# A fused attention and FFT-gate kernel: 128-row position tiles, a forward DFT in four column groups, and six fixed load buffers

## The chip, the cores and the metric

One core of one Trainium2 chip. The metric is the device time of one execution in microseconds (us), lower is better. The kernel before took 247.44 us (median of 3 runs, 246.96 to 247.74). Runs labelled slow (1.5% or more above the fastest of the same kernel) are left out of every ratio.

Engines: PE is TensorE, DVE is VectorE, ACT is ScalarE, POOL is GpSimd, SP is SyncE. PE, DVE and ACT compute, POOL issues the loads from HBM, and SP issues stores and DMA transposes. PSUM is the memory that PE writes its results to, and copying a result out of it is called an eviction. The granted clock is the share of PE's full clock that the profile shows it was given.

## The reference, cut to what matters

```python
# 8 batches, 8 heads, 576 positions, 64 features a head, model width 512
q_p, k_p = phi(q), phi(k)              # relu(x) * (cos, sin) of the position
kv  = k_p^T v ; z = sum(k_p)           # per batch and head, 128 x 64
att = (q_p kv) / (q_p z + 1e-6)        # [576, 512] a batch
x1, x2, x3 = att @ w_proj, split       # 512 -> 3 x 512
y   = x1 * irfft(rfft(x2) * rfft(filter)) * x3     # along the 576 positions
out = y @ w_out
```

The kernel works through the batches with two or three of them in flight. One batch in the words of the traces: load q, k, v; `kp`, `qp` (phi, on DVE) and `va` (a copy of v, on ACT); `kv`; `qpt` (q_p transposed, so that PE can use it as weights); `num` and `att`; `fx` (the first stage of the DFT); `xt` (att transposed); `x2`; `dft`; `x0`/`x2` of the gate, from `xt`; `inv`, `y`, `out`. The moment at which the `kv` of a batch starts is the milestone that I use throughout. Batches are counted from 0.

## The kernel before: the parts that matter

Two tensors have to be transposed in every batch. Batches 0 and 1 do it on PE, with evictions by ACT and DVE. Later batches use DMA transposes, issued by SP:

```python
XT_DMA = (2, 3, 4, 5, 6, 7)     # batches whose xt is a DMA transpose
DMA_QT = 2                      # first batch whose qpt is one
# ... in emit_qt(b, hp), four calls a batch
if b >= DMA_QT:
    nc.sync.dma_start_transpose(out=..., in_=qp[...])       # 2 heads
    return
# ... otherwise PE transposes into PSUM, then an ACT and a DVE copy
# ... in emit_fx: the batch that is not in XT_DMA gets xt from extra matmuls
for dst, gs in ((fx, slice(0, 12)), (xt_t.get(b), slice(12, 24))):
    if gs.start and b in XT_DMA:
        continue
```

Loads go to a rotating pool of four buffers of 96 rows with 6 slots of 64. A load waits for the reader of the tile four loads back:

```python
rw = work.tile([NP, NH, NJ * D], FP16, tag="raw", bufs=4, name=f"{nm}raw{b}")
# ... k and v: one DMA each; q of batch 2 and later: three DMAs
```

The DFT of a batch is nine matmuls of 96 output rows. The last batch evicts its five output tiles in pieces to ACT and DVE, and both SP and ACT issue the stores.

Of the kernel before, what the change touches and what calls it, by code (L numbers as in the profile page):

```python
# [17 lines left out]
def kernel(  # L18
# [25 lines left out]
    NJ, NP = 6, 96  # L44
    NT = 6
# [11 lines left out]
    R3 = math.sqrt(3.0) / 2.0  # L57
# [11 lines left out]
    ccol = consts.tile([128, NJ], FP32, tag="ccol", name="ccol")  # L69
    scol = consts.tile([128, NJ], FP32, tag="scol", name="scol")  # L70
    tcol = consts.tile([128, NJ], FP32, tag="tcol", name="tcol")
    tcol_m = consts.tile([128, NJ], FP32, tag="tcol_m", name="tcol_m")
    epsc = consts.tile([128, NT], FP32, tag="epsc", name="epsc")
    ident = consts.tile([NP, NP], FP16, tag="ident", name="ident")
    swap = consts.tile([NP, NP], FP16, tag="swap", name="swap")
    half_pi = consts.tile([128, 1], FP32, tag="half_pi", name="half_pi")
    m_half_pi = consts.tile([128, 1], FP32, tag="m_half_pi", name="m_half_pi")
    m_pi = consts.tile([128, 1], FP32, tag="m_pi", name="m_pi")
    m_half = consts.tile([128, 1], FP32, tag="m_half", name="m_half")
    wr_col = consts.tile([128, 1], FP32, tag="wr_col", name="wr_col")  # L80
    fm = consts.tile([128, 24, 8], FP16, tag="fm", name="fm")
    tre = consts.tile([NP, 3, NP], FP16, tag="tre", name="tre")
    tim = consts.tile([NP, 3, NP], FP16, tag="tim", name="tim")


    tpad = [consts.tile([128, NP], FP16, tag=f"tpad{i}", name=f"tpad{i}") for i in range(7)]


    ire = consts.tile([NP, 4, QS], FP16, tag="ire", name="ire")
    iim = consts.tile([NP, 4, QS], FP16, tag="iim", name="iim")  # L90
    h3 = consts.tile([NP, 3, 3, DM], FP16, tag="h3", name="h3")
    wp16 = consts.tile([128, NC, 3 * DM], FP16, tag="wp16", name="wp16")
    wo16 = consts.tile([128, NC, DM], FP16, tag="wo16", name="wo16")
# [3 lines left out]
    qpt_buf = [consts.tile([128, NH * S], FP16, tag=f"qpt{i}", name=f"qpt{i}") for i in range(1)]  # L97
    va_buf = [consts.tile([NP, NH, NJ, 66], FP16, tag=f"va{i}", name=f"va{i}") for i in range(2)]
# [4 lines left out]
    def tsc(out, in0, s1, op0, s2=None, op1=None):  # L103
        if op1 is None:
            return nc.vector.tensor_scalar(out=out, in0=in0, scalar1=s1, scalar2=None, op0=op0)
        else:
            return nc.vector.tensor_scalar(out=out, in0=in0, scalar1=s1, scalar2=s2, op0=op0, op1=op1)  # L107

# [14 lines left out]
    XT_DMA = (2, 3, 4, 5, 6, 7)  # L123
    DMA_QT = 2

    def load_qk(b, nm, hs=slice(0, NH)):
        src = {"q": q, "k": k, "v": v}[nm]
        if hs.start == 0:
            rw = work.tile([NP, NH, NJ * D], FP16, tag="raw", bufs=4, name=f"{nm}raw{b}")
            raw_t[(b, nm)] = rw  # L130
        rw = raw_t[(b, nm)]
        view = src[b, hs].rearrange("h (p j) d -> p h (j d)", j=NJ)
        if nm == "q" and b >= DMA_QT:
            nc.gpsimd.dma_start(out=rw[:, hs, 0 : 3 * D], in_=view[:, :, 0 : 3 * D])
            for x in range(2):
                nc.gpsimd.dma_start(
                    out=rw[x::2, hs, 3 * D : 6 * D], in_=view[1 - x :: 2, :, 3 * D : 6 * D]
                )
        else:
            nc.gpsimd.dma_start(out=rw[:, hs], in_=view)  # L140
# [36 lines left out]
    def emit_iotas(part):  # L177
        if part == 0:
            iota("p_i", [128, 1], lambda t: [(t, [[1, 1]], 0, 1)])
            iota("s6_i", [128, NJ], lambda t: [(t, [[1, NJ]], 0, 6)])  # L180
            iota("orow_i", [128, 16], lambda t: [(t, [[1, 16]], 0, 0)])
            iota("nrow_i", [NP, NP], lambda t: [(t, [[1, NP]], 0, 0)])
            return
        iota("fr_i", [NP, 3, NP], lambda t: [
            (t[:, 0], [[3, NP]], 0, 0),
            (t[:, 1], [[6, 48], [4, 2]], 1, 0),
            (t[:, 2], [[6, 48], [2, 2]], 2, 0),
        ])
        iota("sg_i", [NP, NP], lambda t: [(t, [[0, 48], [-2, 2]], 1, 0)])
        iota("s3_i", [128, 3], lambda t: [(t, [[1, 3]], 0, 3)])  # L190
        iota("sr_i", [NP, QS], lambda t: [
            (t[:, ds(j * 48, 48)], [[12, 2], [192, 3], [24, 8]], 2 * j + 1, 0) for j in range(3)
        ])

    def emit_cols():
        p = cc["p"] = small("p")
        nc.vector.tensor_copy(out=p, in_=cc["p_i"])
        nc.vector.memset(half_pi, PI / 2.0)
        nc.vector.memset(m_half_pi, -PI / 2.0)
        nc.vector.memset(m_pi, -PI)  # L200
        nc.vector.memset(m_half, -FX / 2.0)
        nc.vector.memset(warm, 0.0)
        for t in tpad:
            nc.vector.memset(t, 0.0)
        sj = cc["s6_i"]
        nc.scalar.activation(out=ccol, in_=sj, func=AF.Sin, scale=-(PI / 2.0) / S, bias=half_pi)
        nc.scalar.activation(out=scol, in_=sj, func=AF.Sin, scale=(PI / 2.0) / S)
        nc.vector.reciprocal(out=tcol, in_=ccol)
        nc.vector.tensor_tensor(out=tcol, in0=tcol, in1=scol, op=AL.mult)
        tsc(ident, cc["nrow_i"], p[0:NP], AL.is_equal)  # L210
        par = cc["par"] = small("par")
        rnd(par, p, 0.5, -0.25)
        nc.vector.scalar_tensor_tensor(
            out=par, in0=par, scalar=-2.0, in1=p, op0=AL.mult, op1=AL.add
        )
        dest = small("dest")
        nc.vector.scalar_tensor_tensor(
            out=dest, in0=par, scalar=-2.0, in1=p, op0=AL.mult, op1=AL.add
        )
        tsc(dest, dest, 1.0, AL.add)  # L220
        tsc(swap, cc["nrow_i"], dest[0:NP], AL.is_equal)

    def emit_cols_m():
        cm = small("cm", NJ)
        sm = small("sm", NJ)
        nc.vector.tensor_copy(out=sm, in_=cc["s6_i"])
        off = small("off")
        tsc(off, cc["par"], -12.0, AL.mult, 6.0, AL.add)
        tsc(sm[:, 3:6], sm[:, 3:6], off, AL.add)
        nc.scalar.activation(  # L230
            out=cm, in_=sm, func=AF.Sin, scale=-(PI / 2.0) / S, bias=half_pi
        )
        nc.scalar.activation(out=tcol_m, in_=sm, func=AF.Sin, scale=(PI / 2.0) / S)
        nc.vector.reciprocal(out=cm, in_=cm)
        nc.vector.tensor_tensor(out=tcol_m, in0=tcol_m, in1=cm, op=AL.mult)

    def emit_pads():
        for va in va_buf:
            nc.vector.memset(va[:, :, :, D : D + 2], 1.0 / A1)

    def emit_fm():

        p = cc["p"]
        side = small("side")
        tsc(side, p, NP / 2 - 0.5, AL.is_gt)
        loc = small("loc")
        tsc(side, side, -2.0, AL.mult, 1.0, AL.add)
        tsc(loc, p, -(NP - 1) / 2.0, AL.add)
        nc.vector.tensor_tensor(out=loc, in0=loc, in1=side, op=AL.mult)
        tsc(loc, loc, (NP - 1) / 2.0, AL.add)  # L250
        li = small("li")
        rnd(li, loc, 1.0 / 8.0, -7.0 / 16.0)
        lo = small("lo")
        nc.vector.scalar_tensor_tensor(
            out=lo, in0=li, scalar=-8.0, in1=loc, op0=AL.mult, op1=AL.add
        )


        row = small("row")
        tsc(row, lo, 12.0, AL.mult)  # L260
        nc.vector.scalar_tensor_tensor(
            out=row, in0=li, scalar=96.0, in1=row, op0=AL.mult, op1=AL.add
        )
        pos = small("pos", NT)
        for t in range(NT):
            tsc(pos[:, t : t + 1], row, float(6 * (t % 2) + t // 2), AL.add)
        tsc(pos, pos, -(S - 1) / 2.0, AL.add)
        tsc(pos, pos, side, AL.mult, (S - 1) / 2.0, AL.add)
        tsc(pos, pos, float(S - 1), AL.min, 0.0, AL.max)
        nc.scalar.activation(out=epsc, in_=pos, func=AF.Sin, scale=-(PI / 2.0) / S, bias=half_pi)  # L270
        nc.vector.reciprocal(out=epsc, in_=epsc)
        tsc(epsc, epsc, EPS, AL.mult)
        orow_i = cc["orow_i"][:, 0:8]
        match = small("match", 8)
        nc.vector.tensor_copy(out=match, in_=orow_i)
        tsc(match, match, lo, AL.is_equal)

        coef = small("coef", 24)
        ph = small("ph", 6)
        for sl, (kk, c0) in enumerate([(0, 0.25), (3, 0.25), (1, 0.25), (1, 0.0), (2, 0.25), (2, 0.0)]):  # L280
# [30 lines left out]
            op=AL.mult,  # L311
        )

    NCOL = 3 * HS

    FX = 65536.0

# [720 lines left out]
```

## Time and profile before

| | before |
|---|---|
| time, median of the first three runs | 247.44 us |
| span of the profiled run | 242.4 us |
| granted PE clock, mean | 0.991 |
| kv of batch 2 / 3 / 7 starts | 67.8 / 91.3 / 188.2 us |
| steady batch, kv to kv | 24.21 us |
| last gate ends / last eviction ends | 231.93 / 238.42 us |

The prediction below shows the busy lines, the stages and the chain of a steady batch. In the timeline of a DMA queue the columns are start, time until the last of the group was issued, queue, line, operation, tiles and how many. Time in which the queue waits between two transposes of a group is counted in.

```profile
47.89 34.62 SPq L555 DMA_TRANSPOSE qpt<-qp  x8
82.56 3.57 SPq L633 DMA_TRANSPOSE xt<-att  x1
```

The first line covers eight q transposes, four of batch 2 and four of batch 3, with a break of 7.3 us between the fours. The same view, asked for each four alone (from 47.5 to 64 and from 70 to 82.54 us):

```profile
47.89 15.55 SPq L555 DMA_TRANSPOSE qpt<-qp  x4
70.78 11.73 SPq L555 DMA_TRANSPOSE qpt<-qp  x4
```

One of the eight takes 1.3 to 6.2 us in the queue, 3.3 on average. The median of all 24 in that run is 1.585 us. Nobody waited for those eight: PE's table of waits has no line with a DMA in it. The windows of the kernel show columns: width, busy us of PE, PEld, DVE, ACT and POOL with instruction counts, granted clock, mean share of the 16 DMA engines, GB/s; a share over 1 means that packets of several queues overlap.

### The profile page before, as it was taken

To read this page: it belongs to the slowest core of one execution; us is meant where nothing else is said; L and a number is where in the kernel's file an instruction comes from. 1 tells how busy PE (TensorE), PEld (TensorE's weight loads), DVE (VectorE), ACT (ScalarE), POOL (GpSimd) and SP (SyncE) were. 2 spreads that over 40 slices of the span, in tenths; PEclk is the share of its full clock that TensorE was granted. 3 is DMA by queue.
4 is the path that set the end of the run, shared out by engine and by line. 5 is a ranking of instruction groups with operands and counts; after the bars stand their busy time and mean duration, and the time that the engine had idled before them with its cause. 6 is when DMAs were issued, how large, how long until landed. Compare 5 with 4: busy or idle time off the path is not lost.

```text
span 242.4 us, 6225 instructions
## 1 busy us (share of the span) xinstructions
PE 218.4 (90%) x2333; PEld 151.2 (62%) x2333; DVE 212.3 (88%) x747; ACT 178.8 (74%) x275; POOL 35.3 (15%) x61
## 2 busy tenths in 40 slices
PE   1197897998988999999999999999999999999991
PEld 0066576655565866686668666866686668645840
DVE  7588999899889999999999999999999597729781
ACT  2354689999897974899488948894889488778731
POOL 8713411330401031002300230010000000000000
PEclk9998899999999999999999999999999999999999
DMA  5999999799999959999999999999495524063315
GB/s 69 158 205 205 205 208 188 110 162 171 146 202 156 167 92 223 158 153 159 208 249 173 144 194 254 192 142 194 107 187 101 153 54 91 5 171 94 106 42 174
DMA packets 76238, 37.39 MB, mean 154 GB/s; under 512 B 55088, under 2 KB 71856, under 8 KB 76208
## 3 DMA queue, kind: packets, MB, share of 16 engines
q0 software_dynamic: 26000, 16.85, 51.2%
q1 hardware_dynamic: 49792, 19.56, 43.0%
q10 hardware_dynamic: 416, 0.59, 0.8%
q8 instruction: 18, 0.29, 0.5%
q14 instruction: 12, 0.10, 0.1%
HBM read 33.69 MB, written 9.44 MB: 178 GB/s over the span
## 4 chain that ended last, share of the span: by engine, by line
PE 76%; ACT 11%; DVE 6%; DMA 4%; issue 1%; POOL 1%; ACTq 0%; POOLq 0%
PE x L713 26%; PE x L648 12%; PE out L785 11%; PE dft L680 6%; PE kv L543 4%; PE num L584 4%; PE fx L611 3%; PE inv L750 3%; PE inv L749 3%; ACT va L145 3%; DMA vraw<-in_v_dram 3%; DVE att L594 2%; PE out L803 2%; PE qt L563 2%; PE num L535 1%
## 5 line engine op out<-in xcount | busy, mean ns | idle before, releaser
L713 PE MATMUL x<-xt,wp 128*128 128x288 f16 x512 | 67.3, 286 | 0.0
L713 PEld LDWEIGHTS <-wp 128*128 128x128 f16 x512 | 48.9, 98 | 13.2 <-issue 0.4
L648 PE MATMUL x<-wp,fx 128*128 128x512 f16 (+1 forms) x160 | 35.4, 381 | 2.2 <-DVE qpt L569 1.6
L666 ACT ACTIVATE x2f<-x 128x1024 f16<-128x1024 f32 (+1 forms) x24 | 21.2, 885 | 17.1 <-PE x L648 17.1
L594 DVE TENSOR_TENSOR att<-num,rcp 96x768 f16<-96x768 f32 x32 | 30.4, 948 | 0.4
L785 PE MATMUL out<-wo,y 128*128 128x512 f16 (+1 forms) x132 | 30.3, 379 | 0.0
L723 ACT CAST x3s<-x 128x576 f16<-128x576 f32 x32 | 20.4, 638 | 8.5 <-PE x L713 8.0
L145 ACT COPY va<-vraw 96x768 f16<-96x768 f16 x24 | 18.7, 844 | 8.8 <-DMA vraw<-in_v_dram 8.8
L685 ACT CAST xf<-dft 96x1024 f16<-96x1024 f32 x24 | 24.1, 1005 | 1.3 <-PE dft L680 1.1
L543 PE MATMUL kv<-va,kp 96*128 96x65 f16 x384 | 16.1, 196 | 9.8 <-ACT va L145 7.9
L626 ACT CAST fx<-fx 128x576 f16<-128x576 f32 x32 | 20.5, 640 | 5.5 <-PE fx L611 5.5
L720 ACT CAST x1s<-x 128x576 f16<-128x576 f32 x32 | 20.5, 639 | 2.3 <-PE x L713 1.1
L543 PEld LDWEIGHTS <-kp 96*128 96x128 f16 x384 | 14.1, 99 | 12.6 <-DVE kp L107 10.9
L648 PEld LDWEIGHTS <-fx 128*128 128x128 f16 (+1 forms) x160 | 12.7, 100 | 14.8 <-issue 2.5
L584 PEld LDWEIGHTS <-qpt 128*128 128x128 f16 (+1 forms) x384 | 16.8, 106 | 8.2 <-issue 3.8
L785 PEld LDWEIGHTS <-y 128*128 128x128 f16 (+1 forms) x132 | 12.4, 98 | 14.6 <-issue 0.8
L738 DVE TENSOR_TENSOR g<-x3s,x1s 128x288 f16<-128x288 f16 x64 | 17.5, 298 | 4.3 <-ACT x3s L723 4.2
L688 DVE TENSOR_TENSOR m<-xf,h 96x1024 f16<-96x1024 f16 x24 | 16.4, 683 | 4.8 <-ACT xf L685 4.5
L764 DVE TENSOR_TENSOR eo<-eq 128x288 f16<-128x288 f16 x64 | 17.5, 299 | 2.5 <-ACT eq L753 2.5
L611 PE MATMUL fx<-fm,att 96*128 96x96 f16 x240 | 16.3, 207 | 3.6 <-DVE att L594 1.8
L584 PE MATMUL num<-kvs,qpt 128*128 128x65 f16 (+1 forms) x384 | 17.5, 200 | 1.9 <-DVE rcp L593 1.1
L611 PEld LDWEIGHTS <-att 96*128 96x128 f16 x240 | 13.6, 98 | 7.8 <-DVE att L594 3.5
(197 smaller groups left out, 422.1 us busy)
## 6 DMA issues: line engine op xcount, KB each, us to landing
out_dram<-os SPq DMA_DIRECT2D x61, 96.0 KB, 2.4
kraw<-in_k_dram POOLq DMA_DIRECT2D x7, 576.0 KB, 10.3
vraw<-in_v_dram POOLq DMA_DIRECT2D x7, 576.0 KB, 8.8
qraw<-in_q_dram POOLq DMA_DIRECT2D x8, 288.0 KB, 7.5
qraw<-in_q_dram POOLq DMA_DIRECT2D x12, 144.0 KB, 7.9
wp<-in_moe_w_proj_dram POOLq DMA_DIRECT2D x3, 512.0 KB, 11.6
out_dram<-os SPq DMA_DIRECT2D x22, 64.0 KB, 2.6
out_dram<-os SPq DMA_DIRECT2D x14, 48.0 KB, 3.1
```

Source lines behind the costliest of these rows:

```text
L145: copy(out=va_buf[b % 2][:, hs, :, 0:D], in_=raw_t[(b, "v")][:, hs].rearrange("p h (j d) -> p h j d", j=NJ),)
L543: nc.tensor.matmul(u[:, h // 4, ds((h % 4) * 65, 65)], kp[:, j, h].rearrange("p a b -> p (a b)"), va[:, h, j, 0:65], start=(j == 0), stop= ...
L584: nc.tensor.matmul(u[0:m, hh, ds(t * 65, 65)], qpt[:, c0 : c0 + 2 * m - 1 : 2], kvs[:, h // 4, ds((h % 4) * 65, 65)], start=True, stop=True,)
L594: mark["att", b, hp] = nc.vector.tensor_tensor(out=att[:, :, ds(hp * 128, 128)].rearrange("p t (h d) -> p h t d", h=2), in0=nv[:, :, :, 0: ...
L611: nc.tensor.matmul(dst.rearrange("p (g e o) -> p g e o", e=2, o=8)[:, :, e], att[:, 2 * j + e, ds(c * 128, 128)], fm[0:NP, gs], start=True ...
L626: mark["fx", b] = nc.scalar.copy(out=dst[:, c].rearrange("p g (j o) -> p j g o", j=3), in_=uf[:, 0:768].rearrange("p (j g o) -> p j g o", ...
L648: nc.tensor.matmul(dst, fx[:, c].rearrange("p g o -> p (g o)")[:, ds(128 * ch, n)], wp16[:, c, ds(DM, DM)], start=(c == cs[0]), stop=(c == ...
L666: mark["x2f", b, bl] = nc.scalar.mul(out=x2f[:, 2 * bl : 2 * bl + n], in_=u[:, 0:n], mul=X2SC)
L685: mark["xf", b, bl] = nc.scalar.copy(out=xf, in_=u[0:NP])
L713: nc.tensor.matmul(u[:, hf, 0:HS], wp16[:, i, ds(w * DM + c * 128, 128)], xt[:, i, ds(6 * hf, 6)].rearrange("p a b -> p (a b)") if b not i ...
L720: mark["x1s", b, c] = nc.scalar.copy(out=x1s, in_=us[0][:, :, 0:HS])
L785: nc.tensor.matmul(us[t], y[:, c, ds(OT[t], nr)], wo16[:, c], start=(c == 0), stop=(c == NC - 1),)
```

## The change

All position tiles become 128 rows: four slots of 128 and a fifth of 64. Tiles of 96 rows leave a quarter of PE's and DVE's rows unused. So `kv` and `num` need 40 matmuls for 48, and DVE needs ten `kp` steps for twelve. The forward DFT becomes matmuls of 32 output rows, four of which run side by side in PE's column groups. Six fixed buffers replace the pool of four, so loads can run further ahead. And `xt` of batch 1 becomes a DMA transpose, which takes work from ACT in the stage where ACT was full. The core of the diff:

```diff
-    XT_DMA = (2, 3, 4, 5, 6, 7)
+    raw_n = [0]
+    XT_DMA = (1, 2, 3, 4, 5, 6, 7)
+    raw_buf = [const(f"raw{i}", [128, NH, NJ * D], FP16) for i in range(6)]
 ...
-            rw = work.tile([NP, NH, NJ * D], FP16, tag="raw", bufs=4, name=f"{nm}raw{b}")
+            raw_t[(b, nm)] = raw_buf[raw_n[0] % len(raw_buf)]
+        nc.gpsimd.dma_start(              # four slots, runs of 1024 bytes
+            out=rw[:, hs, 0 : 4 * D],
+            in_=src[b, hs, 0:NM].rearrange("h (p j) d -> p h (j d)", j=4),
+        )
+        nc.gpsimd.dma_start(              # fifth slot, runs of 256 bytes
+            out=rw[0:64, hs, 4 * D : 5 * D], in_=src[b, hs, NM:S].rearrange("h p d -> p h d")
+        )
 ...
+            for comp, tab, c0 in ((0, fcos, 0), (1, fsin, 32)):
+                for x in range(4):
+                    nc.tensor.matmul(u[ds(32 * x, 32), comp, 0:n], st, mv, start=True, stop=True)
 ...   # last batch: all tiles up to the last column group, then the last one
+            emit_out(b - 1, OG, range(3))
+            emit_out(b - 1, OG, range(3, 4))
```

## The prediction

> **What bounds the kernel now.** I read the page's busy lines first, then the table of windows cut by stage, then the chain of waits inside one batch, then the start and the end in the timeline. The stretches are mine: the first gate starts at 30 us, ACT is saturated to 62, a steady batch runs from kv to kv (24.2 us).
>
> ```profile
> PE 218.4 (90%) x2333; PEld 151.2 (62%) x2333; DVE 212.3 (88%) x747; ACT 178.8 (74%) x275; POOL 35.3 (15%) x61
> ...
> 37.50:45.00 7.50, 5.91 (x89) 4.45 (x87) 7.50 (x23) 7.50 (x13) 0.77 (x1) 1.00 1.33 180
> 52.00:62.00 10.00, 8.68 (x73) 5.07 (x72) 10.00 (x29) 10.00 (x17) 0.88 (x1) 1.00 1.38 180
> 67.00:74.00 7.00, 5.09 (x115) 4.34 (x112) 6.35 (x24) 6.63 (x11) 0.02 (x1) 1.00 1.46 185
> 115.60:139.80 24.20, 24.20 (x271) 17.08 (x272) 23.55 (x75) 19.15 (x29) 3.54 (x6) 1.00 1.22 193
> 232.00:242.40 10.40, 5.19 (x28) 1.90 (x25) 4.30 (x10) 1.69 (x4) 0.00 (x0) 0.94 0.44 126
> ```
>
> The columns after the width are the busy us of PE, PEld, DVE, ACT, POOL. Three regimes. In a steady batch PE is busy 24.20 of 24.20 with DVE only 0.65 behind. From 37 to 62 us ACT and DVE are full and PE waits. In the last 10 us nobody is busy: that is latency. So 88% busy DVE is worth nothing in the middle and something at the start. The chain inside a steady batch prices PE's work:
>
> ```profile
> 115.60 1.63 PE kv L543 x48
> 117.23 1.73 PE x L648 x8
> 118.96 0.80 PE num L584 x24
> ...
> 121.88 0.66 PE dft L680 x3
> 122.54 0.40 PE num L584 x12
> 122.94 0.55 PE x L648 x4
> 123.50 0.78 PE dft L680 x3
> 124.27 1.96 PE x L713 x16
> 126.23 0.65 PE dft L680 x3
> 126.89 0.26 PE fx L611 x6
> ...
> 135.80 3.46 PE out L785 x16
> 139.25 0.56 PE out L803 x8
> ```
>
> No wait lies between these pieces; they add to 24.2. A 512-column matmul costs 0.216, one of 288 0.122, one of 65 about 0.033.
>
> **What the Trainium skill says, and the trace.**
> (1) "TensorE: Matmul & The Clock Gate", section Back-to-back issue gap: a warm stream costs columns over 2.4 GHz plus 2.5 ns. 512 gives 215.8 ns; the trace has 3.46/16 = 216. Agrees, so I use it for the new widths, 144 (62.5 ns), 160 (69) and 128 (56).
> (2) "TensorEngine Tiling (Array Packing)", Key Properties: tiles run independently, and changing the tiling mode drains TensorE. The last x2 block shows both: four 512-column matmuls in two column groups took 0.55, not 0.86, but above the 0.43 of two; and the next DFT block took 0.78 where its sisters take 0.66. So each change of mode costs about 0.12 us in this trace. No part of this kernel yet runs four groups.
> (3) "DMA: Bandwidth & Descriptors", Specifications: at least 512 B for line rate. The change cuts a k or v row run from 1536 B to 1024 B plus runs of 256 B. What that costs no run here shows.
>
> **The change part by part.**
>
> *PE, per steady batch.* kv and num go from 48 to 40 matmuls each: 8 x 0.032 and 8 x 0.033, -0.26 and -0.26. fx keeps 24 matmuls but they widen from 96 columns to 144 (16 of them) and 160 (8): 4 x (4 x 0.0625 + 2 x 0.069) = 1.55 against 4 x 0.26 = 1.04, +0.51. inv: 16 of 144 and 8 of 288 for 32 of 144, 1.98 for 2.00. Gate, x2 and out keep their columns. DFT: 9 matmuls of 512 (1.95 without the drain) become 16 of 512 and 8 of 128 with 32 columns of weights each. If four groups do run together the array time is 0.43 + 0.43 for the two large blocks, plus the second half of a block that the scheduler splits (below) 0.22, plus about 0.2 for the small one, some 1.25. But the instruction order built for the changed kernel puts two cosine matmuls, then the last ten num matmuls, then the other six: it splits the first block. Mode changes per batch rise from 4 to 10, 6 x 0.12 = +0.72. So -0.70 + 0.72: nothing. The split has a reason: the first block now reads four x2f chunks, so both evictions; before it read two chunks. The second eviction (1.03 us) begins when the last x2 matmul ends; num (0.33), two DFT (0.45) and num (0.33) cover 1.1 us of about 1.35. I charge +0.2. Sum: -0.26 - 0.26 + 0.51 - 0.02 + 0.02 + 0.2 = +0.2 per batch, over five steady batches and the last +1.0 us. The steady stage does not gain.
>
> *DVE, per batch.* kp 12 to 10 operations (2 x 0.26 at issue rate): -0.5; qp: relu 2 x 0.47 to 1 x 0.75 and 6 to 5 scales, -0.45; att 768 to 640 elements at 948 ns: 4 x -0.13 = -0.5; DFT products on three blocks of 1024 to two and one of 256, about -1.2; g one operation for two, 4 x -0.14; the y product split in two, 4 x +0.18. About -2.6 of 23.5. Hidden behind PE there, not at the start.
>
> *ACT, 31 to 62 us.* This is a queue without a gap (DVE too). In issue-rate cost, what disappears: the four xt copies of batch 1, now a DMA transpose, 4 x 0.53 = 2.1; filter-table evictions 6 x 0.5 + 0.5 to 2 x 0.92 + 0.4, -1.2; the third xf, -0.6; va of batches 1 and 2, 8 x -0.13 = -1.0; the extra inverse row, -0.3; and sines now placed ahead of the gate, -2.0. ACT falls from 31 to about 24. PE in the same stretch: h from 27 to 12 large matmuls plus 72 small ones of about 0.03, -1; fx of batch 1 8 x 0.26 to 4 x 0.39, -0.5; kv and num -0.5; 27 becomes 25. DVE 31 becomes 25 to 26 (the itl table adds 8 x 0.2). So the three limits lie at 24 to 26 and the stretch should end near 57 to 58 rather than 62.4. I take -5. From 67 to 74 the y chain and the att operations on DVE bind: +0.7 and -0.5; the batch after has 17.0 PE in 17.4. I add -0.8 for smaller DVE backlog.
>
> *0 to 30 us.* Each load is two DMAs, POOL issues one in 0.67, and there are more iotas ahead of v: v is issued about 1 us later, and v releases the first va at 8.9. Against it, DVE no longer stands behind an ACT sine that itself stood behind that va (2.47 idle), and the kp loop has ten steps for twelve. But scheduled order now has the second half's q scaling before the first att, and five sines before the last xt copy. I take 0, with 1.3 either way.
>
> *The end.* Before, the groups run one after another after the last y, 15 stores in 48-row pieces alternate on two queues, and ACT, which also issues stores, idles 3.85 before one half and 0.87 before the next. After, only the last c is left when y is done at about 233.7: four matmuls and one packed pair, 1.2 us; five 0.4 DVE evictions with ACT beside; five or six stores whose last is issued near 237, plus 2.3 to land. -2.3 us.
>
> Sum: +1.0 - 5.0 - 0.8 + 0 - 2.3 = -7.1, against the measured 247.4: 240.3.
>
> **The rivals.**
> *Four groups do not overlap.* Then the DFT is 16 x 0.216 + 8 x 0.056 = 3.9 instead of 1.95 and each batch gains 2 to 2.7: the kernel goes to about 255. For it: no four-group run in this trace. Against it: the two-group evidence, and out's packed 256-column matmuls, 0.56 for eight where serial would be 0.87.
> *DMA becomes the bound.* Loads rise from 3072 runs a batch (k and v 96 x 8 each, q twice that in its swapped halves) to 4608 (three times 128 x 8 + 64 x 8) and transposes grow by 640/576, 11%. For it: the DMA row is 9 nearly everywhere and its share is 1.1 to 1.2. Against it: over 1.5 occurs in a short window, GB/s reaches 290 around 122 us against 193 over the batch, PE waits for no DMA in a steady batch, and six fixed buffers let a load start a batch earlier than four rotating ones. If it binds: 245 to 252.
> *DVE was the hidden bound and PE's own work is smaller than I think* (the drain in four groups cheaper, the x2f stall covered): steady batch 23.6, total near 236.
> *The startup gain is eaten:* the schedule puts PE's long in-order queue behind a late load; then only the end remains, 245.
>
> **Range and chances.** Startup is uncertain by 2.5, the steady batches by 0.35 x 6 = 2, the end by 1; together about 3.3, plus the DMA tail. 80% range: 235.5 to 245.2. Faster by 2% means under 242.5 (247.44 x 0.98), 2.2 above my centre or two thirds of that spread: 0.73. Within 2%: 0.22. Slower: 0.05, the four-group and DMA rivals.
>
> **What would show it.** Right: a steady kv-to-kv period of 24.2 to 24.6 with PE still full, DVE 21 and ACT 18 inside it; dft lines totalling near 2 us a batch in pieces of 2 and 6; fx 0.39 each; the second x2 stage starting near 57; the last store landing 2 us earlier relative to the end of the gate. Wrong: a period under 23.8 or over 25, waits of PE on x2f evictions over 0.5 us a batch, waits on qpt, xt or raw loads, or a first kv later than 14 us.

## More of the kernel before

```profile
45.00:60.00 15.00, 14.08 (x150) 8.57 (x147) 14.33 (x44) 15.00 (x25) 4.36 (x5) 1.00 1.15 144
60.00:75.00 15.00, 12.13 (x180) 8.46 (x177) 13.03 (x43) 12.55 (x20) 3.80 (x5) 1.00 1.40 173
75.00:100.00 25.00, 25.00 (x274) 17.50 (x274) 24.83 (x78) 18.48 (x27) 2.77 (x4) 1.00 1.05 156
```

In these windows of the kernel, from 45 to 60 us PE, DVE and ACT are nearly full, and from 60 to 75 us they are busy for 81 to 87%. The DMA engines are full in both.

## The result, and the profile after

The changed kernel took 254.19 us (median of 4 runs, 252.79 to 254.64) against 247.2 us for the kernel before on the same chip (4 runs, 244.33 to 247.74). The ratio of fast runs is 1.031, 95% interval 1.023 to 1.039: slower. Ratios here and below are the mean time of one kernel's fast runs over that of the other's fast runs of the same rounds, so they are not quite the ratio of the medians.

The milestones divide the 10.5 us between the two profiled spans (242.4 and 252.9) into stages. They are the starts of the first `kv` matmuls in PE's timeline:

| stage | before | after | difference | predicted |
|---|---|---|---|---|
| start to kv of batch 2 | 67.82 | 62.23 | -5.59 | -5.0 |
| kv 2 to kv 3 | 23.50 | 38.35 | **+14.85** | -0.8 |
| kv 3 to kv 7, four steady batches | 96.84 | 96.57 | -0.27 | +0.8 |
| kv 7 to the end | 54.24 | 55.75 | +1.51 | -2.1 |

The predicted column is the prediction's own terms; its +1.0 for the steady stage is split into four batches and the last one. One stage carries everything. The gain of the compute work was there at 62 us, to 0.6 us, and in the next 38 us more than twice as much was lost. The same windows as before:

```profile
45.00:60.00 15.00, 13.79 (x198) 7.49 (x197) 13.52 (x46) 13.38 (x21) 4.93 (x7) 1.00 1.52 173
60.00:75.00 15.00, 6.73 (x114) 5.14 (x112) 8.43 (x30) 7.63 (x12) 5.02 (x6) 0.71 1.49 150
75.00:100.00 25.00, 19.13 (x151) 12.22 (x148) 17.03 (x56) 12.37 (x20) 1.77 (x2) 0.77 1.40 174
```

From 60 to 75 us every compute engine is half idle and only the DMA engines are full. The chain of waits names what they were waiting for (start, length, what):

```profile
36.53 12.04 DMA raw<-in_v_dram
48.65 2.60 ACT va L149 x4
...
54.34 10.73 DMA qpt<-qp
65.07 17.88 DMA xt<-att
82.99 3.90 PE x L604 x16
87.61 1.96 PE x L604 x16
```

The gate of batch 1 (`PE x L604`, the last two lines) needs `xt` of batch 1. That is the transpose which the change moved to the DMA. It stood behind the q transposes of batch 2, and then took 17.9 us itself. The first 16 gate matmuls took 3.90 us, the next 16 took 1.96: PE had been idle so long that its clock had fallen. The Trainium skill, "TensorE: Matmul & The Clock Gate", section HAM oscillation, describes this: idle gaps throw PE back to half clock until it has been busy again for a while. This trace agrees, with a granted clock of 0.71 from 60 to 75 us, 0.50 from 70 to 83, and a doubled first group.

SP's queue shows the rest of it:

```profile
46.78 18.23 SPq L447 DMA_TRANSPOSE qpt<-qp  x4
65.07 10.25 SPq L520 DMA_TRANSPOSE xt<-att  x1
75.42 18.26 SPq L447 DMA_TRANSPOSE qpt<-qp  x4
```

Four q transposes take 18.2 us, where the kernel before took 15.6 for batch 2 and 11.7 for batch 3. The last one of batch 2 landed 67.6 us into the run before, and 74.4 us after. The `num` of batch 2, which uses them, began at 70.2 us before, so it found them ready, and at 64.4 us in the changed kernel. So the transposes come later and the compute engines come earlier. And `xt` of batch 1 is one transpose more. In PE's table of waits the two DMA lines, absent before, stand first and third:

```profile
PE num L472 <- DMA qpt<-qp: 7.6, 2, 4.9
...
PE x L604 <- DMA xt<-att: 5.9, 1, 5.9
PE out L671 <- ACT os L699: 2.5, 2, 2.0
```

The steady batch, by contrast, is as predicted, 24.14 us:

```profile
124.79 1.38 PE kv L435 x40
126.17 1.73 PE x L541 x8
127.89 0.61 PE num L472 x20
...
131.35 0.61 PE dft L580 x6
131.95 0.55 PE x L541 x4
132.51 0.55 PE dft L580 x8
```

Eight DFT matmuls of 512 columns take 0.55 us here. One after another they would take 8 x 0.216 = 1.73 us. So four column groups do run together.

Loads moved the same 16.85 MB in 40064 packets instead of 26000. The queue with the transposes and stores moved 21.31 MB instead of 19.56.

### The profile page after: what moved, and what is told of

The parts are those of the page before. It is cut to its first block, busy times and chain, and to the rows that moved or that the text cites. A ratio compares the mean times of both kernels' runs of the same rounds, so it can differ in the third digit from the quotient of the medians.

```text
span 252.9 us, 5925 instructions
## 1 busy us (share of the span) xinstructions
PE 216.1 (85%) x2278; PEld 144.4 (57%) x2278; DVE 192.7 (76%) x660; ACT 168.8 (67%) x264; POOL 49.4 (20%) x79
## 3 DMA queue, kind: packets, MB, share of 16 engines
q0 software_dynamic: 40064, 16.85, 54.6%
q1 hardware_dynamic: 55152, 21.31, 45.7%
## 4 chain that ended last, share of the span: by engine, by line
PE 64%; DMA 19%; ACT 9%; DVE 4%; POOL 2%; issue 1%; ACTq 0%; POOLq 0%
PE x L604 23%; PE out L671 11%; PE x L541 10%; DMA xt<-att 7%; DMA raw<-in_v_dram 5%; DMA qpt<-qp 4%; PE dft L580 4%; PE fx L499 3%; PE inv L621 3%; PE kv L435 3%; PE inv L625 3%; DMA raw<-in_k_dram 3%; ACT x2f L559 2%; DVE kp L109 2%; PE out L677 2%; PE fx L505 1%
## 5 line engine op out<-in xcount | busy, mean ns | idle before, releaser
L604 PE MATMUL x<-xt,wp 128*128 128x288 f16 x512 | 68.9, 291 | 5.9 <-DMA xt<-att 5.9
L604 PEld LDWEIGHTS <-wp 128*128 128x128 f16 x512 | 50.1, 99 | 21.4 <-DMA xt<-att 6.8
L671 PE MATMUL out<-wo,y 128*128 128x512 f16 x128 | 29.6, 379 | 2.5 <-ACT os L699 2.5
L609 ACT CAST x2s<-x 128x576 f16<-128x576 f32 x32 | 20.5, 640 | 11.3 <-PE x L604 11.3
L609 ACT CAST x0s<-x 128x576 f16<-128x576 f32 x32 | 20.6, 645 | 10.8 <-PE x L604 9.2
L482 DVE TENSOR_TENSOR att<-num,rcp 128x640 f16<-128x640 f32 x32 | 26.2, 822 | 0.6
L472 PE MATMUL num<-kvs,qpt 128*128 128x65 f16 x320 | 15.1, 198 | 10.7 <-DMA qpt<-qp 7.6
L582 ACT CAST xf<-dft 128x1024 f16<-128x1024 f32 (+1 forms) x24 | 19.1, 802 | 4.8 <-PE dft L580 4.1
L149 ACT COPY va<-raw 128x640 f16<-128x640 f16 x24 | 16.6, 746 | 6.2 <-DMA raw<-in_v_dram 6.2
L631 ACT CAST eq<-inv 128x576 f16<-128x576 f32 x32 | 18.3, 672 | 0.0
L702 ACT ACTIVATE os<-out 128x1024 f32<-128x1024 f32 x14 | 14.6, 1039 | 4.9 <-PE out L671 4.1
L109 DVE TENSOR_SCALAR kp<-raw,ccol 128x512 f16<-128x512 f16 (+1 forms) x45 | 16.9, 376 | 1.2 <-DMA raw<-in_k_dram 1.2
```

Of the source, the lines that this page charges most:

```text
L109: return nc.vector.tensor_scalar(out=out, in0=in0, scalar1=s1, scalar2=s2, op0=op0, op1=op1)
L472: nc.tensor.matmul(u[:, hh, ds(t * 65, 65)], qpt_buf[:, h, ds(t * 128, 128)], kvs[:, h // 4, ds((h % 4) * 65, 65)], start=True, stop=True,)
L482: mark["att", b, hp] = nc.vector.tensor_tensor(out=att[:, hp].rearrange("p t (h d) -> p h t d", h=2), in0=nv[:, :, :, 0:D], in1=rcp.unsque ...
L582: mark["xf", b, bl] = nc.scalar.copy(out=xf, in_=u[:, :, 0:n])
L604: nc.tensor.matmul(u[:, hf, 0:HS], wp16[:, i, ds(w * DM + c * 128, 128)], xt[:, i, ds(HS * hf, HS)], start=(i == 0), stop=(i == NC - 1),)
L609: mark[f"x{w}s", b, c] = nc.scalar.copy(out=x, in_=u[:, :, 0:HS])
```

## The experiments

Three theories were on record at first. T1: the route is wrong, `xt` of batch 1 stands behind the q transposes of batch 2. T2: six buffers let the loads run ahead, and they crowd the transposes. T3: the 256-byte runs of the fifth slot slow the DMA. T4 was formed on the way, and later split into T4a and T4b. Seventeen kernels ran. All give the right result unless I say otherwise. The kernel before ran beside each group, and its medians there were 244.6 to 246.4 us. The changed kernel itself ran in the first comparison alone, so a time set against its 254.19 us is a comparison across rounds; the ratios are to the kernel before in the same rounds.

### xt of batch 1 back on PE, and fewer buffers

```diff
-    XT_DMA = (1, 2, 3, 4, 5, 6, 7)
+    XT_DMA = (2, 3, 4, 5, 6, 7)
-    emit_xt(1)
+    emit_xt(1, (0, 1)); emit_xt(1, (2, 3))        # on PE
```

> The changed kernel, with only the transposed att of batch 1 made on PE and copied by ACT, as batch 0 has it. Theory 1 (the route: that transpose now stands in the transfer queue behind the four of qpt and the first gate of batch 1 waits for it until 83.0 us): the gate then starts right after the second DFT block, near 77 us, and the kernel takes 248 us. Theory 2 (six raw buffers let loads run ahead and slow every transpose): the num of batch 2 still waits for qpt until 74, and the time stays at 251 or more, most of the loss remaining at the qpt waits. Theory 3 (the 256-byte runs make the loads slower): like theory 2.

Measured: 251.24 us median (248.12 to 252.84), ratio 1.022 [1.011, 1.032], unclear. The gate of batch 1 started at 75.5 us instead of 83.0, as T1 says. But the wait came back one batch later:

```profile
84.77 17.73 DMA xt<-att
102.55 2.13 PE x L604 x16
```

Now `xt` of batch 2 stood behind the q transposes of batch 3. The q transposes of batch 2 took 18.4 us in the queue and those of batch 3 took 17.9. kv of batch 3 started at 92.5 us, kv of batch 4 at 118.4. So T1 is true of the place where the wait shows, but not of its cause: the transposes themselves are slow.

The next two kernels tried four fixed buffers instead of six, alone and with the edit above:

```diff
-    raw_buf = [... for i in range(6)]
+    raw_buf = [... for i in range(4)]
```

> The changed kernel with four fixed raw buffers for six, nothing else. Theory 2: loads of batches 3 and 4 no longer run beside the transposes; the four qpt transposes of batch 2 land in under 8 us each rather than 10 to 15, xt in under 9 rather than 17.9, and the time falls to 246 to 249. Theory 1: transposes still take 4 us each in the queue, the gate of batch 1 starts after 80 us, 253 to 255. Theory 3: as theory 1, or slower, because the later loads arrive late.

> Both edits. Theory 1: as with the first edit alone, about 248. Theory 2: as with the second alone, 246 to 249. If both causes add: 244 to 245, which is what the compute saved at the start alone would give.

Both gave a wrong result (relative error 0.47 in the first), at 267.84 and 262.27 us, and are no test of T2. My reading is that with fixed buffers the loads of batch 1 are emitted before the readers of batch 0, so they overwrite data that is still needed. No run shows this. The old kernel with a pool of six was not run.

### The old kernel with one part of the change

```diff
-    XT_DMA = (2, 3, 4, 5, 6, 7)
+    XT_DMA = (1, 2, 3, 4, 5, 6, 7)
     emit_num(1, 3)
+    emit_xt(1)
```

> The kernel before, with only the xt of batch 1 moved to a DMA transpose. Theory 1: the same wait appears in the old kernel; its gate of batch 1 starts at 80 us or later for 75.8, and it takes 251 to 253. Theory 2 and 3: with four buffers and long runs nothing is lost, 246 to 248 (four ACT copies fewer, no gain as the y chain on DVE follows).

Measured: 249.59 us median, but from 243.93 to 251.76. The one fast run took 243.93 us, as little as the kernel before. The profiled run (span 247.0, against 242.4 for the kernel before) is labelled slow, and I draw only one thing from it, with that caution. The gate of batch 1 was not late (74.0 us, before 75.7), and kv of batch 3 started at 89.6 us, earlier than in the old kernel. So in this run of the old kernel the moved transpose alone did not bring the wait that T1 announced. The profile also has 30.5 us between the kv of batches 5 and 6, where 24.2 is the rule, but no fast run was profiled, so this says nothing about the edit.

### Pacing the loads as the old pool did

From batch 2 on, a load takes the buffer that a rotation of four would have given it, so it waits for the same reader as in the old kernel.

```diff
-            raw_t[(b, nm)] = raw_buf[raw_n[0] % len(raw_buf)]
+            if b < 2: ...                                     # as before
+            else:
+                raw_t[(b, nm)] = raw_t[(b - 2, "v") if nm == "q" else (b - 1, "q" if nm == "k" else "k")]
```

> The changed kernel, but from the third batch on a load takes the buffer that the old kernel's rotation of four would give it (the q of a batch waits for the reader of v two batches back, k for the reader of the last q, v for the reader of the last k), so the prefetch no longer runs a batch ahead. T2 (the six buffers let the loads crowd the early DMA transposes): the q transposes of the third batch take 1.5 to 2.5 us each instead of 4.5, PE's waits on qpt in 62-75 us go below 2 us, the kernel comes to 245-249. T1 (the transposes of that stage are slow beside whatever loads there are, and xt of batch 1 stands in their queue): issue times stay above 3.5 us each, the kernel stays at 252-255. If the pacing merely moves the wait, PE waits on raw loads or va later and the time is 254-258.

Measured: 253.86 us, ratio 1.041 [1.033, 1.049], unclear. The four q transposes took 19.4 us in the queue, kv of batch 3 started at 100.8 us. T2 falls: the further prefetch of six buffers is not what makes the transposes slow. That the old kernel, with its pool of four, has transposes of up to 6.2 us in the same stretch points the same way.

### Without the small runs

The fifth slot is not loaded but zeroed, so the result is wrong.

```diff
-        nc.gpsimd.dma_start(
-            out=rw[0:64, hs, 4 * D : 5 * D], in_=src[b, hs, NM:S].rearrange("h p d -> p h d")
-        )
```

> The changed kernel without the loads of the fifth slot (64 rows, 256-byte runs); the slot is zeroed, so the result is wrong on purpose. It takes away 11% of the bytes loaded and a third of the runs and half of the load instructions. T3 (small runs are what slows the DMA): the main loads land in 60-70% of their time, the q transposes of the third batch take under 3 us each, the kernel comes to 244-248. T1 and T2 (transposes beside loads are slow whatever the runs are): 250-253, the gain in proportion to the bytes, transposes still above 3.5 us each.

Measured: 252.77 us, ratio 1.038 [1.031, 1.045], unclear. The four transposes of batch 2 still took 19.1 us. The next four took 9.2 instead of 18.3. kv of batch 3 started at 97.9 instead of 100.6 us, but kv of batch 2 had already come at 58.9 instead of 62.2. From kv 2 to kv 3 it took 39.0 us, against 38.4 in the changed kernel. So without the small loads (11% of the bytes, half of the load instructions) nothing of the 14.9 us comes back, and T3 falls for this stage.

### The early transposes off the DMA

```diff
-    XT_DMA = (1, 2, 3, 4, 5, 6, 7)
-    DMA_QT = 2
+    XT_DMA = (2, 3, 4, 5, 6, 7)
+    DMA_QT = 4
```

> The changed kernel with the q transposes of batches 2 and 3 and the xt of batch 1 on PE with evictions by ACT and DVE, as batches 0 and 1 have them. All theories that put the loss in the early DMA transposes: no PE wait on qpt or xt before 120 us, the kv of batch 3 starts at 93-96 instead of 100.65 (PE work grows by 2 x 40 x 0.06 + 1.2 = 6 us, so not all of 9 us comes back), 248-251 in all. If instead the loss is in the loads themselves (raw buffers), PE then waits on DVE/raw and the time stays at 254.

Measured: 248.12 us (247.23 to 249.03), ratio 1.018 [1.011, 1.024], unclear, where the changed kernel had 1.031. PE waits for no DMA before 120 us, and kv of batch 3 starts at 93.6 us, inside the expected 93 to 96. It is not the whole gain: kv of batch 2 starts at 67.6 us, where the changed kernel had 62.2. My reading is that PE, ACT and DVE now do the transposes in the stage where they were the limit.

### The transposes without loads beside them

T4, from what was known by now: the DMA engines are full or nearly so from 15 to 95 us in both kernels (the old one has gaps near 45 and 88 us), and a transpose is slow because loads run beside it. This kernel drops all loads from batch 3 on (wrong result) and keeps everything else.

```diff
+        if b >= 3:
+            return
         rw = raw_t[(b, nm)]
```

> The changed kernel without any load from the fourth batch on (the old data is used again, so the result is wrong on purpose). Theory T4, formed from the runs so far: the DMA engines are full from 15 to 95 us in both kernels, and a q transpose of that stage takes 4.5 us because loads run beside it. Then without the loads of the fourth and fifth batch the four q transposes of the third batch take 1.3 to 2.5 us each once the loads of batch 2 have landed near 49 us, PE's waits on qpt and xt in 60-83 us are under 2 us together, and the kv of the fourth batch starts at 90-93 us instead of 100.65; the whole kernel 242-246. If the transposes are slow by themselves at this place (their form, or the queue that issues them): still 18 us for four, and kv no earlier than 98.

```profile
45.61 6.42 SPq L449 DMA_TRANSPOSE qpt<-qp  x4
52.08 2.77 SPq L522 DMA_TRANSPOSE xt<-att  x1
65.93 6.88 SPq L449 DMA_TRANSPOSE qpt<-qp  x4
```

Measured: 240.31 us (two runs), ratio 0.979 [0.969, 0.989], unclear. The same four transposes take 6.4 us instead of 18.2, `xt` of batch 1 2.8 instead of 10.3, from the same queue, at the same place, of the same form. kv of batch 3 starts at 86.1 us. That is 5.2 us before the old kernel, against the -5.8 that the prediction's first terms give. T4 holds: the lost time goes with loads and transposes that slow each other. That the loads are slowed too shows in the kernel with the early transposes on PE: its load of q of batch 4 landed 11.8 us after its issue at 48.4 us, where the changed kernel's, issued at 48.7, took 21.3. The old kernel without these loads was not run, so how much it would have gained is not known. The Trainium skill, "DMA: Bandwidth & Descriptors", section Issuing engines are not separate DMA queues, says that DMAs issued by different engines run on the same 16 DMA engines and interleave. This pair of runs agrees: transposes issued by SP go from 1.6 to 4.6 us each when POOL's loads run.

### The same work in another order

The open question was then whether pacing can bring the gain back with all loads in place (T4a, the order costs) or not (T4b, the amount costs). In these kernels the loads of batch n+2 truly depend on the last `att` of batch n: DVE writes a few bytes into the buffer after that `att`, and the load, which overwrites them, has to wait. All three carry the tail changes of the next section too.

```diff
+    def emit_gated_dma(b):
+        for nm in "qkv":
+            with behind("att", b - 2, 3):
+                nc.vector.memset(raw_t[(b - 2, nm)][0:64, 0, 4 * D - 2 : 4 * D + 2], 0.0)
+        emit_input_dma(b)
 ...
     emit_num(n, 3)
     emit_xt(n)
+    if n + 2 < B:
+        emit_gated_dma(n + 2)
```

The first two differ in where DVE scales q of batch 3: after the first y (A), or where the changed kernel has it (B).

> The changed kernel with the loads of batch n+2 held until the last att of batch n is written (a tiny write into the buffer by DVE after that att, so the load truly depends on it); the scaling of q of batch 3 later, after the first y; and the tail changes (group after group to its end, four output tiles). Theory T4a (order is what costs): the four q transposes of batch 2 take 6-9 us together, xt of batch 1 lands before 60 us, PE waits on qpt/xt in 60-83 us are under 1.5 us, kv of batch 3 starts at 87-91 us, the end is 52-53 us after the last kv; 238-242 in all. Theory T4b (the amount of DMA work is what costs): the transposes are fast, but then PE or DVE waits for the raw loads of batch 3 or 4, kv of batch 3 starts no earlier than 95 us, and the time is 248 or more.

> As the run before, but the scaling of q of batch 3 where the changed kernel has it, ahead of the first y on DVE. T4a: as above or up to 2 us better, since q of batch 3 is transposed earlier; but if its load lands later than 62 us, DVE stands in its queue for up to 4 us and the y chain behind it, kv of batch 3 at 90-94 us. T4b: as above.

Measured: A 253.95 us, ratio 1.031 [1.024, 1.037]; B 248.96 us, ratio 1.007 [1.000, 1.013]. In both, the q transposes of batch 2 were fast (6.3 and 5.7 us for four). But `xt` of batch 1 came behind them just as the held loads of batch 3 set in at 51 us. It held the queue for 8.7 and 7.3 us and landed near 68 us in both, not before 60 as T4a expected. kv of batch 3 started at 93.6 and 95.0 us, and PE's wait moved elsewhere. Behind two of B's largest waits stand the late loads of batch 3: DVE and ACT met them in the middle of their queues.

```profile
PE num L478 <- DVE rcp L487: 5.0, 1, 5.0
PE dft L586 <- ACT xf L588: 3.6, 1, 3.6
```

In A the scheduler put `xt` of batch 2 ahead of the q transposes of batch 3, which were issued only at 87.5 us and came late for `num` of batch 3. The third kernel moves both stalls out of the way (q scaled after the second y, v copied where other batches do it). The fourth also takes `xt` of batch 1 off the DMA.

> The gated kernel (loads of batch n+2 held until the last att of batch n; tail changes) with the scaling of q of batch 3 behind the second y of batch 0 and the v copies of batch 3 where other batches have theirs, so that neither DVE nor ACT stands for a load of batch 3. T4a (order): the 5.0 us PE wait on DVE rcp and the 3.6 us on ACT xf vanish, kv of batch 3 starts at 87-90 us instead of 95.1, 240-243 in all. T4b (amount): q of batch 3, transposed 72-85 us beside loads of batch 4, becomes the next wait (PE num on qpt, over 3 us), kv of batch 3 at 91-95 us or a stall right after it, 245-249.

> As the run before, with xt of batch 1 on PE and ACT (1.2 us of PE and 2.2 of ACT more before 60 us). T4a: no gain over the run before, or 1 us lost. T4b: the loads of batch 3 land some 3 us sooner, and the time falls by 1-3 us against the run before.

Measured: 248.42 us, ratio 1.013 [1.007, 1.019], same, and 250.38 us, ratio 1.027 [1.018, 1.036], unclear. In the third kernel kv of batch 3 starts at 85.2 us, better than in any other run, and then kv of batch 4 only at 115.2, 30 us later. Its chain in that stretch:

```profile
79.50 17.70 DMA qpt<-qp x2
...
107.45 17.00 DMA xt<-att
```

The q transposes of batch 3 now ran beside the loads of batch 4, 17.6 us for four, and `xt` of batch 3 beside those of batch 5. So the collision was moved by one batch and not removed. T4a falls for the four orders that I tried: none keeps the gain. T4b fits the first three in the main. The fourth was to be 1 to 3 us faster than the third by T4b, and at most 1 us slower by T4a; it was 2 us slower, which neither expected, and I leave it open. So what is shown is only this: with all loads and all transposes on the DMA, every order that I tried loses time in some batch, in A and in the third kernel also late in the run (26.7 and 27.7 us from kv 6 to kv 7). Whether a cleverer order exists was not shown.

### The end

The end was to be 2.3 us shorter and was 1.5 longer. The chain after the last gate, first of the kernel before:

```profile
232.49 1.69 PE out L785 x7
...
234.20 0.70 DVE os L105
...
238.04 0.38 ACT os L823
```

and of the changed kernel:

```profile
241.34 2.70 PE out L671 x12
244.04 0.45 PE out L677 x6
244.49 0.34 PE out L671
...
244.85 0.43 DVE os L107
...
249.01 0.38 ACT os L699
```

From the end of the gate (231.93 and 240.78 us) the first eviction starts after 2.3 us before, and after 4.1 us in the changed kernel. PE first makes three quarters of all five tiles. Then come single matmuls, each of which waits for the eviction of the other tile in its PSUM unit (the third line in the table of waits above). The first edit puts both tiles' matmuls ahead of their evictions.

> The changed kernel; in the last output stage the matmuls of both tiles of a PSUM unit come before their evictions. If the sharing of a unit between two tiles costs the end (PE out waits of 0.48 and 2.02 us on ACT evictions of the other tile): the stretch from the last kv to the end falls from 31.5 to 29-30 us, the kernel to 252. If stores or evictions bound the end anyway: no change within 0.5 us.

Measured: 254.59 us, no change, and the last eviction ended 8.7 us after the gate instead of 8.6. The waits on evictions were gone. In their place the chain had a 2.62 us wait for a store, since the output tile has three buffers and the last batch needs four. The next kernel adds a fourth buffer, on top of the early transposes on PE:

```diff
-    ... tag="os", bufs=3, ...
+    ... tag="os", bufs=4, ...
```

> The kernel with the early transposes on PE (q of batches 2 and 3, xt of batch 1), plus in the end: both tiles' matmuls of a unit before their evictions, and four instead of three output tiles in SBUF, so that no eviction waits for a store. The run with the tail change alone showed the wait for a store (2.62 us) in place of the waits for evictions. If these two are all that holds the end: from the last kv to the end 53 us instead of 55.7, the kernel at 245-246. If another wait takes their place: 248.

Measured: 247.75 us, ratio 1.009 [1.003, 1.016]. From the last kv to the end 55.4 us instead of 55.8, so the expected 53 was missed. Last came the order itself, in the changed kernel with the two edits above:

```diff
-            emit_out(b - 1, OG, range(3))
-            emit_out(b - 1, OG, range(3, 4))
+            for grp in OG:
+                emit_out(b - 1, (grp,))
```

> The changed kernel with the tail changes alone: out's groups of the last batch one after another, each to its last column group, both tiles' matmuls before their evictions, four output tiles in SBUF. In the changed kernel PE makes three quarters of all five tiles first and the first eviction starts 4.1 us after the gate's end. If this order costs the end: first eviction of the last batch 2.3 us after the gate's end, the last store issued 5.5-6.5 us after it instead of 8.6, so 2-3 us less: 251-252. If the evictions and stores themselves bind: less than 1 us.

Measured: 252.85 us, ratio 1.024 [1.020, 1.029]. From the last kv to the end 54.4 us, 1.4 less than the changed kernel and about as long as the kernel before (54.2). The last eviction ends 6.7 us after the gate instead of 8.6. The two earlier edits gave 0.4 us of this in the run before, so about 1.0 of the 1.5 us that the tail had lost goes to the order of the last matmuls. The runs do not show a tail that is shorter than the old one.

### The repairs together

```diff
+    XT_DMA = (3, 4, 5, 6, 7) ; DMA_QT = 3     # q of batch 2, xt of 1 and 2 on PE
             emit_num(n, 3)
+            emit_dft(b, (0,))                  # the first DFT block after all of num
```

> As the run before, but q of batch 3 by DMA again and xt of batches 1 and 2 on PE, so one transposition of 40 on PE less and one of 20 more; and the first DFT block after the whole of num, so that it isn't split into 2 and 6. If the early DMA transposes are the loss, four of them (q of batch 3) alone have 20 us to run in and land in time: kv of batch 3 starts at 92-93 us. Each mode change costs some 0.12 us: two fewer make the steady period 23.9 instead of 24.14; if the split covered a wait for the x2f eviction instead, the period stays or grows to 24.4. In all 242-244 if both hold, so about the same as the kernel before.

This kernel also has the first two tail edits. Measured: 247.60 us, ratio 1.008 [1.000, 1.016]. kv of batch 3 starts at 93.2 us. The steady period stays at 24.14 to 24.19 us, although the block is no longer split. In its place PE waits up to 0.2 us a batch for the x2f eviction. So the split cost nothing that its removal gave back. With the output groups one after another as well:

> q of batch 2 and xt of batches 1 and 2 on PE, first DFT block after num, output groups one after another with four output tiles. The parts were measured apart: 247.6 with the earlier tail, and the tail change is worth about 1 us more (54.3 against 55.3 us from the last kv to the end). If they add: 246.3 to 246.8, within 1% of the kernel before and 3% below the changed one, not faster than the old. If the tail waits for stores again: 247.5.

Measured: 246.65 us (six runs, 246.27 to 247.04), ratio 1.007 [1.002, 1.012]. That is the lowest median of a correct version of the new layout, 2 to 3% below the changed kernel (2.3% by the ratios 1.007 and 1.031, 3.0% by the medians of different rounds) and within 1% of the old one. No correct version beat the kernel before.

## Why the prediction was wrong, point by point

*0 to 62 us* (predicted 0 and -5.0). Right, and where it was expected: kv of batch 1 came 0.6 us earlier, and another 5.0 us were gained from there to kv of batch 2, 5.6 in all. The second x2 stage started near 57 us as announced (56.3).

*The stretch behind it* (predicted -0.8). This is the step that failed: it measured +14.85 us. The prediction took the y chain and the att operations on DVE for the limit of that stretch and had no DMA term in its sum. In its place PE waited for q transposes (7.6 us in all) and for `xt` (5.9 us) that ran beside loads. Without loads from batch 3 on, kv 2 to kv 3 took 22.8 us instead of 38.4. It knew the rival ("DMA becomes the bound", 245 to 252) and named its sign, waits on qpt, xt or raw loads, and exactly that sign came, though 254 us lies above the 245 to 252 that it was given. It was argued away by three readings. "PE waits for no DMA in a steady batch" was true, but looked at the wrong stage. "Over 1.5 occurs in a short window" took a share near 1.4 for slack, while four transposes took 15.6 us beside it. And "six fixed buffers let a load start a batch earlier" counted as relief, while starting earlier was no gain (the paced run changed nothing). The view that would have told it was there before the change: eight transposes of 3.3 us on average in SP's queue, against 1.6 for the sixteen after them. Nothing waited for them because the compute engines came later: the last one of batch 2 landed at 67.6 us, and its reader began at 70.2. That the transposes then got slower still (18.2 us for 15.6 and 11.7) was not foreseen. Without the small loads those of batch 3 took 9.2 us and those of batch 2 still 19.1, so for batch 2 the reason stays open. The moved `xt` of batch 1 was priced as 2.1 us of ACT work gained, and its cost on the DMA as none; it held its queue for 10.3 us and landed 17.9 us after its issue.

*Steady batches* (predicted +0.2 each). Right in substance: 24.14 us against 24.21, just under the announced 24.2 to 24.6, DVE 21.26 and ACT 18.15 busy where 21 and 18 were announced. One citation of the prediction is to be read with care: Back-to-back issue gap, in "TensorE: Matmul & The Clock Gate" of the Trainium skill, calls columns over 2.4 GHz plus 2.5 ns the gap of an isolated matmul and has about 131 ns for a sustained stream of 512 columns; the 216 ns of the trace before, in a run of 16, agree with the formula. The rival "four groups do not overlap" is out.

*The end* (predicted -2.3). Wrong: +1.5 for the stage from the last kv. "Only the last c is left when y is done" overlooked PE's order. More than twenty matmuls stand between the gate and the first eviction of the last batch, and tiles that share a PSUM unit alternate with evictions. Reordered, it measured 54.4 us, where before has 54.2.

*The range* (235.5 to 245.2). It left no room for the rival, which got some of 5%. The run without loads came to 240.31 us, just the predicted 240.3, but that is luck. In its rounds the kernel before took 245.49 us, so it gained 5.2 us and not 7.1. By its stages it gained 4.5 us up to kv 2 and 0.7 from there to kv 3, much as the sum has it, and lost 1.4 at the end, where the sum has a gain. So the compute terms up to kv 3 were right for a kernel whose DMA is not in the way.

## What to carry to other kernels

A speed-up of the compute engines brings forward every transfer that they trigger or wait for. So look in the profile before the change at transfers that are slow while nobody waits for them: they are the next bound, and their slack is what the gain may use up. Moving work from a full engine to a DMA queue has to be priced at the rate that transfers have in that stage, not at their best rate. When a wait goes away under an edit but the time does not, follow it one batch further before calling it solved.

## What the Trainium skill lacked or had wrong

- "DMA: Bandwidth & Descriptors", section Latency and other measured facts, gives 261 GB/s for a DMA transpose with a non-contiguous middle dimension. With hardly a load beside it, this case shows 204 GB/s for q (128 x 1280 elements of two bytes, 327,680 bytes, in 6.42/4 us) and 237 GB/s for `xt` (655,360 bytes in 2.77 us), worked out from issue times: near it. From the first issue to the last landing, four q transposes took 8.33 us, which makes 157 GB/s. The page has no figure for a transpose beside loads. Here it is 72 GB/s for q (18.23/4 us) and 64 GB/s for `xt` (10.25 us).
- The same page, Issuing engines are not separate DMA queues, is confirmed. It has no figure for the loss: here the transposes took 2.8 to 3.7 times as long, and a load of q 21.3 us for 11.8.
- "TensorEngine Tiling (Array Packing)" has no cost for a change of tiling mode. The prediction took 0.12 us from the old trace, and eight four-group matmuls of 512 columns took 0.55 us where two rounds of 0.216 make 0.43. But taking one split, and so two changes, out of a batch left the period at 24.14 us or more, since a wait for an eviction took their place.
